# A gated mix of a state-space layer and a dense layer: a new start-up, a new order of the first stages and a split last chunk

## The chip, the cores and the metric

The kernel runs on one core of one Trainium2 chip. The metric is the device time of one execution in microseconds (us). The kernel before took 234.26 us (median of 3 runs, 233.33 to 234.62).

The core has a matrix engine (TensorE, in the profile PE, with its weight loads as PEld), VectorE (DVE), ScalarE (ACT), GpSimd (POOL) and SyncE (SP). SP, ACT and POOL issue loads; all loads run on 16 DMA engines. In what follows a "stage" is one use of TensorE on one block of 512 rows of x.

## The reference, cut to what matters

```python
g = sigmoid((x * gate_w).sum(-1, keepdims=True))             # x: 2048 x 640
# a: a diagonal complex state-space layer
Bu = einsum("bld,pd->blp", x, B_bar)                          # state projection
h[t] = Lam_bar * h[t-1] + Bu[:, t]                            # scan over 2048 steps
a = 2 * einsum("blp,dp->bld", h, C).real + x * Dskip          # output projection
# b: a dense layer
b = gelu(x @ w1 + b1) @ w2 + b2                               # 640 -> 1728 -> 640
return g * a + (1 - g) * b
```

Everything is bf16 outside and accumulates in fp32. The kernel cuts the rows into 4 blocks of 512 (`q`), 8 scan blocks of 256 (`b`) and 16 output chunks of 128 (`c`).

## The kernel before: the parts that matter here

The kernel is written as a list of operations, each with an engine, an estimated duration, the tiles that it reads and writes, and a priority. A small list scheduler, run when the kernel is built, turns this into one fixed instruction order per engine. So an engine can stand behind an operation whose data is late, even if the next one could run.

The loads, and the first block of x, which is transposed by TensorE and copied from PSUM by VectorE and ScalarE in turn:

```python
xnload(0, prio=0)                                  # x block 0, 640 KB, SyncE
W1P = [(0, 256), (256, 896), (896, F)]             # first-layer weights in three pieces, SyncE
# ... small rows of parameters on ScalarE's queue ...
load("b2",  "pool", ...)
load("dsk", "pool", "l_dsk", dsk[:, :], A_Dskip.partition_broadcast(128), ["dsk"], prio=-29, dur=1.0)
load("gwb", "pool", "l_gwb", gwb[:, :], gate_w.partition_broadcast(128), ["gwb"], prio=-28, dur=1.0)
for c in range(4):
    op(f"tp{c}", "pe", 0.5, [("xn", 0), "ident"], [("bank", bank)], f_tp, prio=-900 + c)
    op(f"tpe{c}", "dve" if c % 2 == 0 else "act", 0.6, [("bank", bank)], [("xT", 0, c)], f_tpe, prio=-900 + c)
# ... angles, sines and tables of the scan on DVE and ACT, priorities -950 to -945 ...
load_T("xT_rest", ..., prio=6)                     # 5 transposing loads, SyncE
load_T("B", ..., prio=7)                           # 10 transposing loads, SyncE
load("w2a", "sp", ..., prio=8); load("w2b", "sp", ..., prio=9)
load_T("C", ..., prio=10)                          # 10 transposing loads, SyncE
```

The stages. `m1` is the first dense layer with its gelu, `bproj` the state projection (evacuated into `U` by ScalarE), `ssm` the scan on VectorE (tiles V, W, G, result H), `gates` the dot product with the gate row, `outs` the second dense layer, the output projection and the mix:

```python
gates(0)
m1(0)
m1(1)
bproj(0)
ssm(0)
ssm(1)
xnload(1, prio=500)          # x block 1, SyncE, after all other loads
gates(1)
bproj(1)
ssm(2)
outs(0)
# ... blocks 2 and 3 ...
```

One output chunk is evacuated twice by ScalarE (E1, E2), added twice by VectorE and stored whole:

```python
t = tt(osb[c % NO][:, :], xg[c % 2][:, :], E1[c % NE][:, :], ALU.add)
E.wait("dve", t)
return tt(osb[c % NO][:, :], osb[c % NO][:, :], E2[c % NE][:, :], ALU.add)
```

## Time and profile before

| What | us | Where it is read |
|---|---|---|
| span of the profiled execution | 231.5 | head of the page |
| TensorE busy | 213.0 (92%) | part 1 |
| first matmul of the first layer | 11.24 | timeline |
| its first 7 matmuls, spacing | 0.42 to 0.43 each | stretches of one tile |
| last matmul done | 227.7 | chain |

From the page of the kernel before: the span, and the busiest engine (busy us, share, instructions).

```profile
span 231.5 us, 3235 instructions
PE 213.0 (92%) x1261; PEld 123.6 (53%) x1272; DVE 189.4 (82%) x263; ACT 102.1 (44%) x173; POOL 2.5 (1%) x11
```

A busy share of 92% says only that TensorE is the engine to watch. What TensorE needs is read from its undisturbed spacing: in the chain of waits 28 matmuls of 320 columns take 3.81 us and, elsewhere, 50 of 512 columns (49 of them recorded) take 10.8 us. Over all 768 of the one and 480 of the other that is 208 us. The rest, some 23 us, is what a change of order can win, and the waits show where it lies. The view of waits of the kernel before (who waited <- for whom: us in total, times, longest):

```profile
DVE scr L571 <- DMA xn<-in_A_x_dram: 16.8, 1, 16.8
...
ACT gth L578 <- DVE scr L571: 8.7, 3, 6.7
...
PE ps L618 <- ACT U L627: 3.9, 1, 3.9
...
PE ps L597 <- DVE xT L403: 2.7, 1, 2.7
...
PE ps L717 <- DVE H L467: 1.6, 2, 1.1
```

The first three lines are one wait seen from three engines. SyncE issued x's second block at 51.2 us, behind all transposing loads. VectorE stood 16.8 us in front of the gate product that reads it. ScalarE stood in front of the tanh of that gate. TensorE stood in front of a PSUM bank that ScalarE had yet to empty. Only the last one, 3.9 us, cost time.

The start, from the timeline of the kernel before (start, duration, engine, line, operation):

```profile
10.70 0.48 DVE L403 COPY xT<-ps 128x640 bf16<-128x640 bf16 x1
...
11.24 11.02 PE L597 MATMUL ps<-xT,W1sb 128*128 128x512 bf16 x43 [2.65 <-DVE xT L403]
```

x landed at 5.1 us, but the third of the four copies of its transpose stood behind the table work on VectorE until 10.7. And the first real matmuls are slow. From the table of stretches of the kernel before, limited to the instructions of W1's tile (stretch, its length, then busy us and count of PE and PEld, granted clock, DMA share, GB/s):

```profile
11.20:14.11 2.91, 2.87 (x7) 1.04 (x8) 1.00 1.23 282
15.20:22.00 6.80, 6.75 (x32) 3.13 (x32) 1.00 1.14 197
```

Seven matmuls in 2.87 us, later 32 in 6.75: twice the speed. The column of the granted clock reads 1.00 in both, because the first clock event in this trace is the release itself, at 14.0 us; before it the spacing is the better witness.

The end, from the chain of waits of the kernel before (start, duration, what):

```profile
224.96 2.73 PE ps L717 x20
227.69 0.02 issue
227.72 0.54 ACT E_1 L725
228.25 0.02 issue
228.28 0.50 DVE osb L467
228.78 0.02 issue
228.80 0.49 DVE osb L467
```

After the last matmul come one evacuation, two adds and a store: 3.8 us to the end of the span.

### The profile page before, as it was taken

The numbers are of one execution on the slowest core, as the hardware profiler recorded it, in microseconds if no ns is written. First come the engines' busy times: TensorE is split into PE (matmuls) and PEld (weight loads), VectorE is DVE, ScalarE is ACT, GpSimd is POOL, SyncE is SP. The second block draws the span as 40 slices with busy tenths as digits, with TensorE's granted clock in tenths as the row PEclk, the third lists the DMA queues.
The fourth block names the chain that finished last, engine by engine and source line by source line (L and its number), as shares of the span: only waits on it lengthen the run. The fifth ranks groups of instructions, "written<-read, shape, count | busy, mean of one in ns | idle before, by whom it ended". The sixth has DMA issues, their size and how long they took to land.

```text
span 231.5 us, 3235 instructions
## 1 busy us (share of the span) xinstructions
PE 213.0 (92%) x1261; PEld 123.6 (53%) x1272; DVE 189.4 (82%) x263; ACT 102.1 (44%) x173; POOL 2.5 (1%) x11
## 2 busy tenths in 40 slices
PE   1499999997599899999999999999999999999993
PEld 0344444443246676554446777644446777777772
DVE  2899997003899999999999999999996999999411
ACT  2656666551552233456553332366553332333231
POOL 4000000000000000000000000000000000000000
PEclk9999999999999999999999999999999999999999
DMA  6999599964000002200000001400000000000100
GB/s 203 325 240 184 122 115 352 169 134 120 0 0 0 3 28 57 84 31 28 0 3 0 0 31 29 142 28 0 3 0 0 3 28 28 31 0 31 57 30 28
DMA packets 29624, 15.45 MB, mean 67 GB/s; under 512 B 21802, under 2 KB 29546, under 8 KB 29610
## 3 DMA queue, kind: packets, MB, share of 16 engines
q1 hardware_dynamic: 29424, 14.91, 25.1%
q0 software_dynamic: 128, 0.33, 0.8%
q8 instruction: 10, 0.16, 0.3%
q14 instruction: 4, 0.03, 0.0%
q10 hardware_dynamic: 58, 0.01, 0.0%
HBM read 7.38 MB, written 2.62 MB: 43 GB/s over the span
## 4 chain that ended last, share of the span: by engine, by line
PE 57%; SPq 21%; DVE 16%; DMA 2%; issue 1%; ACT 1%
PE ps L693 20%; SPq L336 20%; PE ps L717 17%; PE ps L597 12%; PE ps L618 9%; DVE G L658 5%; DVE V L467 3%; DVE H L467 3%; DVE W L467 2%; DMA xn<-in_A_x_dram 2%; SPq L329 2%; DVE scr L571 1%; DVE osb L467 1%; DVE xg L733 1%; ACT U L627 0%
## 5 line engine op out<-in xcount | busy, mean ns | idle before, releaser
L597 PE MATMUL ps<-xT,W1sb 128*128 128x512 bf16 (+1 forms) x273 | 62.2, 385 | 3.0 <-DVE xT L403 2.7
L693 PE MATMUL ps<-W2sb,Gl 128*128 128x320 bf16 x448 | 63.4, 299 | 0.0
L693 PEld LDWEIGHTS ps<-W2sb,Gl 128*128 128x128 bf16 x448 | 43.8, 98 | 17.6
L604 ACT ACTIVATE Gl<-ps,b1col 128x512 bf16<-128x512 f32 (+1 forms) x56 | 38.5, 687 | 23.9 <-PE ps L597 23.9
L717 PE MATMUL ps<-CT,H 128*128 128x320 bf16 x320 | 45.9, 299 | 1.6 <-DVE H L467 1.6
L618 PE MATMUL ps<-xT,BT 128*128 128x512 bf16 x196 | 43.5, 379 | 4.2 <-ACT U L627 3.9
L597 PEld LDWEIGHTS ps<-xT,W1sb 128*128 128x128 bf16 (+1 forms) x280 | 27.4, 100 | 37.1 <-issue 3.9
L658 DVE TENSOR_TENSOR_SCAN G<-atab,V 128x1280 bf16<-128x1280 f32 x16 | 44.3, 2811 | 0.3
L717 PEld LDWEIGHTS ps<-CT,H 128*128 128x128 bf16 x320 | 31.1, 98 | 14.5 <-DVE H L467 2.4
L618 PEld LDWEIGHTS ps<-xT,BT 128*128 128x128 bf16 x200 | 19.2, 97 | 28.3 <-issue 5.6
L627 ACT ACTIVATE U<-ps 128x512 bf16<-128x512 f32 x40 | 23.3, 595 | 14.9 <-PE ps L618 14.9
L571 DVE SCALAR_TENSOR_TENSOR scr<-xn,gwb 128x640 bf16<-128x640 bf16 x16 | 13.2, 823 | 17.3 <-DMA xn<-in_A_x_dram 16.8
L701 ACT ACTIVATE E_1<-ps,g1col 128x320 bf16<-128x320 f32 x16 | 8.4, 527 | 22.0 <-PE ps L693 20.3
L701 ACT ACTIVATE E_0<-ps,g1col 128x320 bf16<-128x320 f32 x16 | 8.4, 527 | 21.8 <-PE ps L693 21.8
L725 ACT ACTIVATE E_0<-ps,gcol 128x320 bf16<-128x320 f32 x16 | 8.4, 527 | 15.1 <-PE ps L717 15.1
L467 DVE TENSOR_TENSOR V<-mr,U 128x2560 bf16<-128x2560 bf16 x8 | 11.9, 1490 | 3.1 <-ACT U L627 2.9
L733 DVE SCALAR_TENSOR_TENSOR xg<-xn,gcol,dsk 128x640 bf16<-128x640 bf16 x16 | 14.0, 883 | 0.5
L725 ACT ACTIVATE E_1<-ps,gcol 128x320 bf16<-128x320 f32 x16 | 8.4, 527 | 13.3 <-PE ps L717 13.3
L467 DVE TENSOR_TENSOR V<-V,W 128x1280 bf16<-128x1280 bf16 x16 | 12.5, 821 | 0.3
L467 DVE TENSOR_TENSOR H<-H,W 128x1280 bf16<-128x1280 bf16 x16 | 12.5, 820 | 0.3
L467 DVE TENSOR_TENSOR H<-c,G 128x2560 bf16<-128x2560 bf16 x8 | 11.9, 1487 | 0.1
L467 DVE TENSOR_TENSOR W<-s,G 128x2560 bf16<-128x2560 bf16 x8 | 11.9, 1484 | 0.0
(78 smaller groups left out, 79.9 us busy)
## 6 DMA issues: line engine op xcount, KB each, us to landing
xn<-in_A_x_dram SPq DMA_DIRECT2D x4, 640.0 KB, 4.3
out_dram<-osb SPq DMA_DIRECT2D x16, 160.0 KB, 1.8
W2sb<-in_B_w_dram SPq DMA_DIRECT2D x1, 2080.0 KB, 9.3
W1sb<-in_B_w_dram SPq DMA_DIRECT2D x1, 1040.0 KB, 10.6
W1sb<-in_B_w_dram SPq DMA_DIRECT2D x1, 800.0 KB, 8.4
W1sb<-in_B_w_dram SPq DMA_DIRECT2D x1, 320.0 KB, 4.8
dsk<-in_A_Dskip_dram POOLq DMA_DIRECT2D x1, 160.0 KB, 7.1
gwb<-in_gate_w_dram POOLq DMA_DIRECT2D x1, 160.0 KB, 7.2
```

The lines of the kernel that those rows point to most:

```text
L336: t = dma_inc("sp", nc.sync.dma_start_transpose(dst, src), sem)
L467: return inc("dve", nc.vector.tensor_tensor(out=o, in0=a, in1=b, op=o_))
L597: t = nc.tensor.matmul(PS[bank][0:n, :], W1sb[:, k, jf * 128:jf * 128 + n], xT[:, k, q * 512:(q + 1) * 512], start=(k == 0), stop=(k == KD ...
L604: return inc("act", nc.scalar.activation(Gl[q % 2][0:n, jf, :], PS[bank][0:n, :], ACT.Gelu_apprx_tanh, bias=b1col[0:n, jf:jf + 1]))
L618: t = nc.tensor.matmul(PS[bank][:, :], BT[:, kd, ci, k * 128:(k + 1) * 128], xT[:, kd, q * 512:(q + 1) * 512], start=(kd == 0), stop=(kd = ...
L627: return inc("act", nc.scalar.activation(dst, src, ACT.Copy, scale=1.0 if ci == 0 else -1.0))
L658: t = inc("dve", nc.vector.tensor_tensor_scan(out=g[:, ci, :], data0=a, data1=v[:, ci, :], initial=0.0, op0=ALU.mult, op1=ALU.add))
L693: t = nc.tensor.matmul(PS[bank][:, 0:HALF], Gl[q % 2][0:n, jf, t4 * 128:(t4 + 1) * 128], W2sb[0:n, jf, cols], start=(jf == 0), stop=(jf == ...
L701: return inc("act", nc.scalar.activation(E1[c % NE][:, cols], PS[bank][:, 0:HALF], ACT.Copy, scale=g1col[:, c:c + 1]))
L717: t = nc.tensor.matmul(PS[bank][:, 0:HALF], H[b % NHB][:, ci, k, s * 128:(s + 1) * 128], CT[:, k, ci, cols], start=(i == 0), stop=(i == 2 ...
L725: return inc("act", nc.scalar.activation(E2[c % NE][:, cols], PS[bank][:, 0:HALF], ACT.Copy, scale=gcol[:, c:c + 1]))
L733: return inc("dve", nc.vector.scalar_tensor_tensor(out=xg[c % 2][:, :], in0=xn[q % 2][:, c % 4, :], scalar=gcol[:, c:c + 1], in1=dsk[:, :] ...
```

## The change

The intent: start TensorE earlier and warm, take the late load of x's second block out of everybody's way, give the scans their input one stage sooner, and shorten the tail. The core of the diff:

```diff
-        xnload(0, prio=0)
+        for h in range(2):                                   # x block 0 in two loads
+            load(f"x0_{h}", "sp", f"l_x0{h}", xn[0][:, 2 * h:2 * h + 2, :], ...)
...
-            load(f"xn{q}", "sp", ...)                        # later blocks of x
+            load(f"xn{q}{tag}", "pool", ..., dur=1.0, lat=6.0)
...
+        def f_warm():
+            t = None
+            for _ in range(7):
+                t = nc.tensor.matmul(PS[BK_C[1]][:, :], wz[:, 0:128], wz[:, :], start=True, stop=True)
+            return inc("pe", t)
+
+        op("warm", "pe", 3.0, ["wz"], [("bank", BK_C[1])], f_warm, prio=-1000)
...
-            op(f"tpe{c}", "dve" if c % 2 == 0 else "act", 0.6, ..., prio=-900 + c)
+            op(f"tpe{c}", "dve", 0.5, [("bank", bank)], [("xT", 0, c)], f_tpe, prio=-2000 + c)
...
-        load_T("xT_rest", ..., prio=6, dur=11.7)
+        load_T("xT_rest", ..., prio=7, dur=13.0)
-        load_T("B", ..., prio=7, dur=13.1)
+        load_T("B", ..., prio=6, dur=13.1)
...
-        gates(0)
         m1(0)
-        m1(1)
         bproj(0)
         ssm(0)
+        gates(0)
+        m1(1)
         ssm(1)
-        xnload(1, prio=500)
-        gates(1)
         bproj(1)
         ssm(2)
+        xnload(1, "g")                                       # on POOL's queue, waits for nothing
+        gates(1)
         outs(0)
```

Cut here: the columns of parameters and of the bias are transposed in two operations instead of one; in blocks 2 and 3 the state projection also comes before the first layer; E1 and E2 get three buffers instead of two, G is folded into W and V; the last chunk reads its output projection straight from PSUM (`out = psum * g + E2`) and is stored in two halves; the scheduler's estimated durations are adjusted. The loads of x's blocks 2 and 3 still wait until their buffer is free.

## The prediction

> **What bounds it now.** TensorE. From 94.7 to 227.7 us the chain of waits is matmuls with nothing between them; VectorE is 98% busy there (table of stretches) but delays nothing. Undisturbed spacing, from the chain: 0.136 us per matmul of 320 columns, 0.2157 per 512. 480 x 0.2157 + 768 x 0.136 = 208 us of streaming in a 231.5 us span. The other 23 us lie in known places:
>
> - start: the first real matmul is at 11.24 us (timeline). x had landed at 5.1, but its third evacuation queued on VectorE behind table work and ended at 11.2 ("DVE xT", 2.7 us in the waits);
> - cold start: 7 matmuls take 2.9 us (0.43 apart), then 0.216: 1.4 us lost;
> - 3.9 us (56.4 to 60.3): the second state projection waits for an evacuation of U. ScalarE stood 6.7 us behind a gate's tanh, that behind the gate product on VectorE, that 16.8 us for x's second block, issued at 51.2 after all transposing loads;
> - 1.1 + 0.5 us: outputs wait for H, because that same wait held the first scan back to 60.6;
> - tail: 3.8 us after the last matmul (0.53 evacuation, two adds of 0.49, store).
>
> **What the change does.**
> 1. Transposes start on half of x; evacuations go first, all on VectorE (0.49 against 0.69 on ScalarE). First matmul at about 7.4 us: -3.8.
> 2. Seven zero matmuls, 3 us while TensorE is idle anyway. The Trainium skill ("TensorE: Matmul & The Clock Gate", Part 1) says that about 3.4 us of activity releases the clock; the trace agrees in size (2.9 us). I count -1.0, as the gap before real work may lose part.
> 3. x's later blocks go early through POOL's queue; gate work moves behind the first scans: the 3.9 us stall and the 1.6 us for H go. First scan at about 37 instead of 60.6: VectorE gets over 15 us of slack. -5.5.
> 4. The last chunk reads PSUM directly and leaves in halves: -1.0.
> 5. More E buffers, G folded into W: off the critical path.
>
> Sum -11.3. **Given back:** TensorE now runs ahead of its loads. In before the second piece of W1 landed at 10.2 us (issue plus time to landing); at a start of 7.4 it is wanted at 9.5: about +1. State projections now follow directly, so B's transposed loads are wanted at about 24 us and the rest of x at 35. In before the first of these 15 transposing loads stood 8 us at issue, the last landed about 35, the DMA being over 100% busy from 4 to 20 us. The order is swapped, not shortened, and x's second block (640 KB) joins that traffic. I expect waits of 1 to 4 us in total before the first state projection and the second first-layer stage: about +2.
>
> Net about -9: span near 222.5. **Predicted time 225 us, 80% range 221.5 to 229.5.** Faster by over 2% (under 229.6): 0.89; within 2%: 0.10; slower: 0.01.
>
> **What would show it.** First matmul with W1 at 7 to 8 us, spaced 0.216 from the start; new TensorE waits of 2 to 4 us on DMA (W1, BT, xT) before 40 us; none on ScalarE's U evacuation, none over 0.5 us on H; VectorE idle over 15 us outside its prelude; the last store under 3 us after the last matmul; matmul time unchanged.
>
> **What would make it wrong.** Transposed loads landing later than about 38 us (each us costs one; 4 us more and the gain is under 3%), or no data wait at all (222). The clock falling back in those waits (+1.4 each). Static order: a gate or an evacuation in ScalarE's or VectorE's queue ahead of its data (x's third block arriving late through POOL) brings a stall like the old one back.

## The result, and the profile after

The kernel after took 226.86 us (median of 4 runs, 225.31 to 227.38) against 234.01 us for the kernel before with the same runs. Ratios here are computed as the mean time of one kernel's fast runs over that of the other's of the same rounds, so they are not quite the ratio of the medians: 0.9684, 95% interval 0.9629 to 0.9739. One run of the kernel before in one group was slow and is left out of the ratios.

The page of the kernel after, the same lines as before:

```profile
span 225.6 us, 3268 instructions
PE 218.3 (97%) x1279; PEld 124.8 (55%) x1279; DVE 191.6 (85%) x267; ACT 101.5 (45%) x170; POOL 4.8 (2%) x14
```

TensorE is busy 5 us longer in a span that is 6 us shorter: 3.2 us of it are the zero matmuls, which do no work for the result; the rest is mostly first-layer matmuls at half speed. The chain of waits of the kernel after:

```profile
2.27 11.59 DMA W1sb<-in_B_w_dram
13.86 0.05 issue
13.91 15.23 PE ps L622 x60
29.14 10.90 PE ps L643 x50
...
220.15 2.73 PE ps L742 x20
222.88 0.03 issue
222.91 0.55 DVE osb L775
```

From 13.91 us to the end TensorE waits for nothing at all. The chain names what came before: a load of W1. The waits of TensorE in the kernel after:

```profile
PE ps L442 <- DMA W1sb<-in_B_w_dram: 1.5, 1, 1.5
PE ps L388 <- DVE wz L381: 1.2, 1, 1.2
PE ps L622 <- DVE tr L474: 1.1, 1, 1.1
PE ps L622 <- DMA W1sb<-in_B_w_dram: 0.7, 1, 0.7
```

The waits for U, for H and for the copy of x are gone. Two of these lines misname their releaser, as the inferred releasers of this view sometimes do. The first layer does not read the tile of "<- DVE tr L474". And L442 transposes the bias rows and does not read W1: the weight load just before it waited 1.7 us for b1rows. The bias rows thus came late too, at 7.5 us, but W1 came later still. When W1 came is shown by the issues of loads. From part 6 of the pages, W1's three pieces before (320, 800 and 1040 KB; the last number is us from issue to landing):

```profile
W1sb<-in_B_w_dram SPq DMA_DIRECT2D x1, 1040.0 KB, 10.6
W1sb<-in_B_w_dram SPq DMA_DIRECT2D x1, 800.0 KB, 8.4
W1sb<-in_B_w_dram SPq DMA_DIRECT2D x1, 320.0 KB, 4.8
```

and after:

```profile
W1sb<-in_B_w_dram SPq DMA_DIRECT2D x1, 1040.0 KB, 13.7
W1sb<-in_B_w_dram SPq DMA_DIRECT2D x1, 800.0 KB, 11.6
...
W1sb<-in_B_w_dram SPq DMA_DIRECT2D x1, 320.0 KB, 6.9
```

With the issue times of the timeline (1.26, 1.80, 2.36 us before; 1.76, 2.27, 2.84 after) the pieces landed at 6.1, 10.2 and 13.0 us before, and at 8.7, 13.9 and 16.5 after. The first real matmul of the kernel after starts at 8.76 us, 0.1 us after the first piece, and its third tile at 13.91, just after the second.

The granted clock and the DMA in that stretch. The table of stretches of the kernel after (stretch, length, busy us and count of PE, PEld, DVE, ACT, POOL, then granted clock, DMA share, GB/s):

```profile
5.00:6.00 1.00, 0.99 (x13) 0.68 (x13) 1.00 (x4) 0.00 (x0) 0.00 (x0) 1.00 0.86 150
6.00:7.00 1.00, 0.00 (x0) 0.00 (x0) 0.52 (x3) 0.21 (x1) 0.00 (x0) 1.00 0.73 127
7.00:8.00 1.00, 0.18 (x1) 0.09 (x1) 0.27 (x3) 0.00 (x0) 0.00 (x0) 0.87 0.99 301
...
10.00:11.00 1.00, 1.00 (x4) 0.43 (x3) 1.00 (x1) 0.00 (x0) 0.00 (x0) 0.50 1.02 389
```

Two things are to be seen. The clock falls to one half between 7 and 8 us, before the first real matmul. And from 5 to 7 us the DMA moves only 127 to 150 GB/s though its engines are 73 to 86% busy, against 389 GB/s later.

The kernel before has such a dip as well, from 6 to 8 us. Its table of stretches:

```profile
6.00:7.00 1.00, 0.38 (x7) 0.39 (x8) 0.46 (x2) 0.00 (x0) 0.00 (x0) 1.00 1.29 193
7.00:8.00 1.00, 1.00 (x12) 1.00 (x11) 0.69 (x5) 0.65 (x2) 0.00 (x0) 1.00 0.69 218
```

There it came when W1's first piece had just landed (6.1 us), and TensorE had no use for W1 before 11.2.

The clock events in the trace say the same more exactly (start, length in us, granted share; times from the span's start):

```
kernel before   14.01  218.45  1.0
kernel after     4.32    3.41  1.0
                 7.73   10.24  0.5
                17.97  208.21  1.0
```

The zero matmuls (1.20 to 4.37 us) did release the clock at 4.32 us, and it was taken back one window of 3.41 us later; TensorE had little but transposes and idle time in that window. It came back after three more windows. The Trainium skill ("TensorE: Matmul & The Clock Gate", Part 1) describes free-running windows of 3,413 ns that grant or take back the clock, and the trace agrees: 3.41 us, and 10.24 us is three times 3,413 ns. That page's Part 4 says of a transpose that "it doesn't count as PE-busy the same way". The traces agree only in part. The window from 4.3 to 7.7 us was busy for 1.8 us, nearly all of it transposes, and lost the clock, while the kernel before kept it through a window with 1.4 us of matmuls (54.97 to 58.38 us, in the wait for U). That fits the page, but the margin is small. For getting the clock back, though, transposes did count: in e8 (below) the window from 3.42 to 6.83 us held 0.95 us of zero matmuls and otherwise transposes and released the clock, while in e2 one with 2.3 us of first-layer matmuls (7.25 to 10.66 us) did not.

Where did the time go? The end of the first layer of block 0 is a good checkpoint, because both kernels do the same work up to it. The weight loads of its last tile begin at 26.72 us before and at 27.87 us after, so **in these two executions the new start-up lost 1.15 us**. All of the gain lies behind it: 3.9 us (U), 1.6 us (H) and 1.1 us (tail: 3.78 us from the last matmul to the end of the span before, 2.69 after). Less the 1.15 us, that makes 5.4 of the 5.9 us between the two spans; the rest are gaps too small to name.

The medians differ by more, 7.15 us, because the profiled execution of the kernel before was its fastest and that of the kernel after its slowest (227.38 us, granted clock 0.977; the others had 0.985 and 0.992). In e6, the same kernel traced again, the clock came back after two windows and not three, and the same point was reached at 26.11 us, 0.6 us before the kernel before. So the start-up brought between -1.15 and +0.6 us, against 3.8 us expected. Behind this point the kernel after takes 197.7 us (e6: 198.4, with one wait of 0.9) and the kernel before 204.8. The traces of e1, e2, e3, e9, e10 and e12 also take 197.7 us there, so what these runs vary is the start alone.

### The profile page after: what moved, and what is told of

It reads as the page before. It is cut to its first block, busy times and chain, and to the rows that moved or that the text cites. A ratio compares the mean times of both kernels' runs of the same rounds, so it can differ in the third digit from the quotient of the medians.

```text
span 225.6 us, 3268 instructions
## 1 busy us (share of the span) xinstructions
PE 218.3 (97%) x1279; PEld 124.8 (55%) x1279; DVE 191.6 (85%) x267; ACT 101.5 (45%) x170; POOL 4.8 (2%) x14
## 4 chain that ended last, share of the span: by engine, by line
PE 93%; DMA 5%; SPq 1%; DVE 0%; issue 0%
PE ps L718 27%; PE ps L622 27%; PE ps L742 19%; PE ps L643 19%; DMA W1sb<-in_B_w_dram 5%; SPq L328 1%; DVE osb L775 0%
## 5 line engine op out<-in xcount | busy, mean ns | idle before, releaser
L622 PE MATMUL ps<-xT,W1sb 128*128 128x512 bf16 (+1 forms) x280 | 65.8, 397 | 1.8 <-DVE tr L474 1.1
L622 PEld LDWEIGHTS ps<-xT,W1sb 128*128 128x128 bf16 (+1 forms) x280 | 28.1, 102 | 38.7 <-issue 6.6
L683 DVE TENSOR_TENSOR_SCAN W<-atab,V 128x1280 bf16<-128x1280 f32 x16 | 44.3, 2811 | 0.3
L742 PEld LDWEIGHTS ps<-CT,H 128*128 128x128 bf16 x320 | 31.3, 98 | 12.3
L652 ACT ACTIVATE U<-ps 128x512 bf16<-128x512 f32 x40 | 23.9, 597 | 19.4 <-PE ps L643 19.4
L726 ACT ACTIVATE E_0<-ps,g1col 128x320 bf16<-128x320 f32 x12 | 6.3, 527 | 16.5 <-PE ps L718 15.1
L492 DVE TENSOR_TENSOR H<-H,V 128x1280 bf16<-128x1280 bf16 x16 | 12.5, 821 | 0.3
L492 DVE TENSOR_TENSOR H<-c,W 128x2560 bf16<-128x2560 bf16 x8 | 11.9, 1489 | 0.2
L492 DVE TENSOR_TENSOR W<-mi,U 128x2560 bf16<-128x2560 bf16 x8 | 11.9, 1484 | 0.0
L492 DVE TENSOR_TENSOR V<-s,W 128x2560 bf16<-128x2560 bf16 x8 | 11.9, 1484 | 0.0
L726 ACT ACTIVATE E_1<-ps,g1col 128x320 bf16<-128x320 f32 x10 | 5.3, 528 | 13.7 <-PE ps L718 13.7
L726 ACT ACTIVATE E_2<-ps,g1col 128x320 bf16<-128x320 f32 x10 | 5.3, 527 | 13.7 <-PE ps L718 13.7
## 6 DMA issues: line engine op xcount, KB each, us to landing
W1sb<-in_B_w_dram SPq DMA_DIRECT2D x1, 1040.0 KB, 13.7
```

What stands on the lines that cost most here:

```text
L492: return inc("dve", nc.vector.tensor_tensor(out=o, in0=a, in1=b, op=o_))
L622: t = nc.tensor.matmul(PS[bank][0:n, :], W1sb[:, k, jf * 128:jf * 128 + n], xT[:, k, q * 512:(q + 1) * 512], start=(k == 0), stop=(k == KD ...
L652: return inc("act", nc.scalar.activation(dst, src, ACT.Copy, scale=1.0 if ci == 0 else -1.0))
L683: t = inc("dve", nc.vector.tensor_tensor_scan(out=g[:, ci, :], data0=a, data1=v[:, ci, :], initial=0.0, op0=ALU.mult, op1=ALU.add))
L726: return inc("act", nc.scalar.activation(E1[c % NE][:, cols], PS[bank][:, 0:HALF], ACT.Copy, scale=g1col[:, c:c + 1]))
L742: t = nc.tensor.matmul(PS[bank][:, 0:HALF], H[b % NHB][:, ci, k, s * 128:(s + 1) * 128], CT[:, k, ci, cols], start=(i == 0), stop=(i == 2 ...
```

## The experiments

The questions: what made W1 late and so ate the start-up's gain; whether the zero matmuls are worth anything; and which part of the change removed the waits for U and H. Twelve more programs ran (two of them repeats), in three groups of four; each group shares its runs of the kernel before (11 runs in each). All gave correct results.

| Run | Kernel | Median us | Ratio to before, 95% interval |
|---|---|---|---|
| | after | 226.86 | 0.9684 (0.9629 to 0.9739) |
| e1 | after, x's block 1 held back | 224.86 | 0.9608 (0.9561 to 0.9654) |
| e2 | after without zero matmuls | 226.43 | 0.9673 (0.9621 to 0.9725) |
| e3 | after with the old order | 225.37 | 0.9632 (0.9588 to 0.9675) |
| e5 | before, x's blocks through POOL | 229.32 | 0.9800 (0.9754 to 0.9846) |
| e6 | after again | 226.37 | 0.9664 (0.9628 to 0.9701) |
| e7 | after, broadcasts held back | 224.36 | 0.9577 (0.9538 to 0.9617) |
| e8 | after, both held back | 223.05 | 0.9530 (0.9495 to 0.9565) |
| e9 | e8 with the old order | 222.50 | 0.9509 (0.9474 to 0.9544) |
| e11 | e8 again | 222.66 | 0.9538 (0.9495 to 0.9580) |
| e10 | e8 without zero matmuls | 223.20 | 0.9563 (0.9515 to 0.9612) |
| e13 | e8 with the old copies of x | 223.02 | 0.9538 (0.9499 to 0.9578) |
| e12 | e9 with filler matmuls | 222.00 | 0.9490 (0.9452 to 0.9529) |

### e5: one part of the change alone, in the kernel before

```diff
-            load(f"xn{q}", "sp", f"l_xn{q}", ...)
+            load(f"xn{q}", "sp" if q == 0 else "pool", f"l_xn{q}", ...)
```

> The kernel before with one change: x's blocks 1 to 3 are loaded through POOL's queue, so block 1 at once instead of after all transposing loads. Theory: this alone takes away the 3.9 us wait for U and most of the 1.6 us for H: 4 to 5.5 us below before (about 229). W1's second piece may land at 13 to 14, which costs nothing here, as it is wanted at about 14.8. Rival (the waits come from the order of the stages): within 1 us of before.

Measured: 229.32 us, 4.9 below the 234.19 that is the median of the kernel before's fast runs in its group. By the 2% rule this is unclear (interval 0.9754 to 0.9846), but it is clear of no change. The waits of TensorE that are left in its profile:

```profile
PE ps L394 <- DMA xn<-in_A_x_dram: 5.1, 1, 5.1
PE ps L597 <- DVE xT L403: 2.7, 1, 2.7
PE ps L415 <- DMA b1rows<-in_B_b_dram: 2.0, 1, 2.0
```

All are at the start; the waits for U and for H are gone. So the earlier load of x's second block accounts for the part of the gain behind the start, but for the tail, and the order of the stages is not needed for it. (Blocks 2 and 3 moved to POOL's queue too, but in the kernel before nothing stood waiting for them: from 94.7 us on its chain is matmuls.) From the end of the first layer of block 0 this kernel takes 199.0 us, 5.7 less than the kernel before; before that point it loses 1.5 us. In this kernel the first layer starts at 12.4 us, later than in the kernel before (11.2), as the small parameter rows come later (2.0 us in the waits against 0.8 before). That fits what e1 found of the load's cost, but it is one trace each. W1's second piece landed at 12.3 us, not at 10.2, and cost nothing here, as expected.

### e3: the old order of the first stages in the kernel after

```diff
         m1(0)
+        m1(1)
         bproj(0)
         ssm(0)
         gates(0)
-        m1(1)
         ssm(1)
```

and the rest of x is again loaded ahead of B.

> The kernel after with the old order of the first stages (first layer of block 0, of block 1, then the state projection of block 0; rest of x loaded ahead of B). Theory: the earlier projection is what took away the waits for H; with the old order the first scan starts near 56 us instead of 45, TensorE waits for H again (1 to 2 us at the first output, up to 4 at the third), and the time is 2 to 5 us above after. Rival: the earlier load of x's second block alone removed those waits; then within 1 us of after.

Measured: 225.37 us. The theory fell and the rival held (0.9632 against 0.9684 and 0.9664 for the kernel after): no wait for H is in the profile, although the first scan starts at 58.4 us instead of 45.2. The first H is complete at about 69.05 us and the first output projection starts at 69.6. The fixed order had put 42 matmuls of the second layer in front of it, not 28. So the swap of the projections buys VectorE slack that is not needed here, though only 0.5 us was left without it. In this trace W1's first piece landed at 7.6 us, but the first real matmul started at 8.79: TensorE's order has the transpose of the bias rows in front, and those came late (2.4 us in the waits).

### e2: the kernel after without the zero matmuls

```diff
-        op("warm", "pe", 3.0, ["wz"], [("bank", BK_C[1])], f_warm, prio=-1000)
```

> The kernel after without the seven zero matmuls. In the profile of after the granted clock was 1.00 until 7.6 us, 0.50 from there to 18.0: the release was lost again before the first real matmul at 8.8. Theory: the zero matmuls buy nothing as long as W1 comes this late; without them the time is within 0.8 us of after. Rival (the warm-up works in most runs, the profiled one was unlucky): 1.5 to 3 us slower than after.

Measured: 226.43 us, ratio 0.9673 against 0.9684 and 0.9664 for the kernel after. As expected, they buy nothing here. In this run's profile the first ten matmuls of the first layer take 4.43 us, as in the kernel after, and end before W1's second piece lands at 14.1.

### e1: x's second block held back

```diff
-        xnload(1, "g")
+        xnload(1, "g", reads=("ptab",))     # the load waits for VectorE's tables, about 37 us
```

> The kernel after, with one change: the early 640 KB load of x's second block on POOL's queue is held back until the VectorE tables are done (about 37 us). Theory A (that load takes DMA share from W1): the second piece of W1, which landed at 13.9 us in the profile of after (10.2 in before), lands at about 11, the first piece at about 7 instead of 8.7, and the time falls by 2 to 3.5 us below after (about 224). Rival B (W1 is late because of B's transposing loads or because it is issued half a microsecond later): W1 still lands at 13 to 14 and the time is within 0.7 us of after.

Measured: 224.86 us, ratio 0.9608; against the kernel after in another group (0.9664) that is 1.3 us of 234, less than the 2 to 3.5 expected and more than the rival's 0.7. (The groups ran on different chips and the two intervals overlap; but every run of e1 is faster than every run of the kernel after.) W1's second piece landed at 11.8 us instead of 13.9. Theory A held for the second piece. It missed for the first: that piece landed at 9.9 us, later than in the kernel after, and now set the start. So x's block is not all that held W1 up: in the kernel before the two pieces landed at 6.1 and 10.2 us.

The packet records of the trace, which tell of each transfer its queue, size, start and duration, showed a candidate. POOL's queue carries, in this order, the broadcasts of the skip row and of the gate row (each one row of 1.25 KB written to 128 partitions, 160 KB) and x's second block. Both appear as packets of 5,120 bytes:

```
kernel after, packets of 5,120 bytes on POOL's queue
broadcasts:        64 packets,  4.64 to  9.10 us, mean 431 ns, longest 1,156 ns
x's second block: 128 packets,  8.89 to 12.83 us, mean 203 ns, longest   371 ns
```

A packet of a broadcast took twice as long, on average, as a packet of the same size of x. Between 4 and 7 us, while they ran, the core moved 127 to 206 GB/s. That the first 64 packets are the broadcasts is inferred from their order and number (320 KB over 5,120 bytes). The place in time does not explain the difference: in e7 (below), where the two changed places, x's packets took 214 ns on average from 5.6 us on and the broadcasts' 382 ns from 38.7 us on.

One thing the packet records also show: the broadcasts are not new. The kernel before issues them at the same time, and its 64 packets run from 5.90 to 9.43 us, 460 ns on average. New is that they now start before W1's first piece has landed: the two kernels with the old start-up have the piece at 6.1 us (e5: 6.0) and the first broadcast packet at 5.9 (5.7), while in the kernel after and e1 to e3 the packets start at 4.6 to 5.1 and the piece lands at 7.6 to 9.9. What moved them forward (x in two loads, W1 issued half a microsecond later, the other order of the transposing loads) was not varied by a run of its own.

### e6, e7, e8: the broadcasts held back, alone and with x's block

e6 is the kernel after, unchanged.

> The kernel after itself, unchanged, as the reference of this group on this chip: about 226.8 us, ratio to before near 0.968; W1's second piece lands between 13 and 14 us in its profile, and the clock record shows a release after the zero matmuls that is lost before the first real matmul.

Measured: 226.37 us, ratio 0.9664. W1's second piece landed at 13.7 us, and the clock was released at 4.33 us, lost at 7.75 and back at 14.57.

e7 moves the two broadcast loads behind the tables; x's block stays early:

```diff
-        load("dsk", "pool", "l_dsk", ..., prio=-29, dur=1.0)
-        load("gwb", "pool", "l_gwb", ..., prio=-28, dur=1.0)
+        load("dsk", "pool", "l_dsk", ..., prio=-29, dur=1.0, lat=7.0, reads=("ptab",))
+        load("gwb", "pool", "l_gwb", ..., prio=-28, dur=1.0, lat=7.0, reads=("ptab",))
```

> The kernel after, with the two broadcast loads (the skip row and the gate row, each 1.25 KB spread over 128 partitions) held back until VectorE's tables are done; x's second block stays early. The packet records of after show 64 packets of 5,120 bytes on POOL's queue between 4 and 8 us that take 0.2 to 0.95 us each, 0.2 us being what the same size costs for x's block later; while they run the core moves 130 to 200 GB/s instead of 390. Theory C (the broadcasts hold W1 up): the dip from 5 to 8 us goes, W1's first piece lands near 6.5 to 7 us and the second near 11 to 12, TensorE's first real matmul starts near 7 to 7.5, and the time is 1.5 to 3.5 us under after. Rival (the dip has another cause, such as the 512-byte rows of W1's first piece): first matmul still after 8.3, time within 0.8 us of after.

Measured: 224.36 us, 2.0 us below e6. The second piece landed at 10.9 us. The first landed at 8.2 us and the first real matmul was at 8.25, so this part of the expectation missed: x's block, now alone on POOL's queue, had moved up to where the broadcasts had been (its packets run from 5.6 us on). And a new wait appeared, the one that the prediction had looked for, 1.6 us for B:

```profile
PE ps L643 <- DMA BT<-in_A_B_im_dram: 1.6, 1, 1.6
```

e8 holds back both.

> The kernel after with both the broadcasts and x's second block held back until the tables are done. Theory: W1's pieces land near 6.5, 9 and 11.5 us, so the first layer of block 0 runs without a stop from about 7 us; then the next limit shows, B's transposed loads, which by the SyncE issue times land near 24 to 25, a wait of 1 to 3 us before the first state projection; net 3 to 5.5 us under after (about 222). Rival (start-up is bounded by something else, such as the cold clock or the bias column): within 1.5 us of the run that holds back only x's block.

Measured: 223.05 us, 3.3 us below e6 (ratios 0.9530 and 0.9664). The three pieces landed at 7.1, 9.2 and 11.8 us and the first layer starts at 7.37. The same rows of the table of stretches as above, for e8:

```profile
5.00:6.00 1.00, 1.00 (x13) 0.80 (x10) 0.92 (x2) 0.00 (x0) 0.00 (x0) 1.00 0.97 177
6.00:7.00 1.00, 0.90 (x9) 0.59 (x8) 0.75 (x3) 0.21 (x1) 0.00 (x0) 1.00 0.95 330
7.00:8.00 1.00, 0.63 (x3) 0.31 (x4) 0.93 (x6) 0.41 (x2) 0.00 (x0) 1.00 1.06 382
```

From 6 us on the core moves 330 GB/s and more until 11 us. The first clock event of this trace is the release, at 6.83 us (the 1.00 in the rows before it is a default), and it is not lost again. So what POOL had issued, the broadcasts and x's second block together, is what kept W1 late in the kernel after: without it the second piece lands even earlier than in the kernel before (10.2 us). Of the two only x's block was added by the change. The kernel before would perhaps gain from later broadcasts too; no run tested that. The low rate from 5 to 6 us stays also without them, so it has another cause; W1's first piece, whose rows are only 512 bytes long, is moving then, but no run tested that.

The expected wait for B was 1 to 3 us. In e8's list of TensorE's waits it does not stand; 0.4 us of it is in that of e11, the same kernel. Two waits put down to ScalarE, 0.9 and 0.7 us, are what is left of the start. Before the first one ScalarE loads its function tables. The second is right in front of the state projection, and B is only just hidden behind it: B's last load landed at 24.25 us, the gelu of the first layer's last tile ended at 24.51.

### e9: both held back, with the old order

> The same as the run before it, with the old order of the first stages (first layer of block 1 before the first state projection, rest of x loaded ahead of B). Theory: loads land in time in this order (rest of x by about 20 us, wanted at 22), so the wait for B goes; but VectorE gets its first work some 15 us later, and waits for H of 0 to 3 us can come back. Between 1.5 us faster and 2 us slower than the run before it.

Measured: 222.50 us, within the noise of e8 (the intervals of 0.9509 and 0.9530 overlap). No wait for H came back, and no wait for a load is left after the start. In the profiled run the clock was released at 4.31 us, lost at 7.72 and back at 11.13; eight or nine real matmuls ran at half speed in between.

### e10, e11, e13: what the zero matmuls and the copies are worth once W1 is on time

e11 is e8 unchanged.

> The kernel that holds back the broadcasts and x's second block, unchanged, as the reference of this group: ratio to before near 0.953, granted clock 1.00 throughout after the zero matmuls.

Measured: 222.66 us, ratio 0.9538. In one of its six runs the granted clock averaged 0.992, so the release can still be lost.

e10 takes the zero matmuls away from it.

> The same without the seven zero matmuls. In the unchanged after they bought nothing, since W1 came too late for the released clock. Theory: with W1 on time they do pay: without them the first 7 or more matmuls with W1 run 0.43 us apart and the time is 1 to 2 us above the reference of this group. Rival (they are worthless anyway, transposes or the first real work release the clock as early): within 0.5 us.

Measured: 223.20 us, ratio 0.9563 against 0.9538: 0.6 us, inside the noise. The theory of 1 to 2 us is not borne out. Its trace shows where the gain ends. Without the zero matmuls the clock came at 10.31 us instead of 5.15, and the first layer lost time. Yet the first state projection starts at 24.34 us in e10 and at 24.39 in e11. From the waits of TensorE in e11:

```profile
PE ps L622 <- ACT Gl L629: 1.0, 1, 1.0
...
PE ps L643 <- DMA BT<-in_A_B_im_dram: 0.4, 1, 0.4
```

With a warm start TensorE just runs into ScalarE and into B's loads sooner.

e13 gives e8 the old copies of x (VectorE and ScalarE in turn, at the old priority).

> The reference of this group with the old evacuation of x (halves shared by VectorE and ScalarE, behind the table work in VectorE's order; x still loaded in two parts). Theory: now that W1 is on time, the evacuation is what the first real matmul waits for: it moves from 7.4 to 9 to 11 us and the time rises by 1.5 to 3.5 us, part of it lost again to the cold clock, part hidden where B's loads are the limit. Rival (W1 still sets the start): within 0.7 us.

Measured: 223.02 us, ratio 0.9538, the same as e11. The expectation missed, and the reason is in the timeline: in this program the fixed order put all four copies ahead of the angle work anyway (the last one ends at 7.39 us, first real matmul at 7.49), probably because the parameters are now transposed after most of x and not before it. So e13 did not bring back the late copy of the kernel before. That the copies cost the kernel before 2.7 us is read from its waits; it was not tested by a run.

### e12: a filler, and the fastest version

Filler on top of e9, between the last transpose of x and the bias column (the expectation's clock times for e9 are 0.3 us later than those above, which count from the span's start):

```diff
+        def f_fill():
+            t = None
+            for _ in range(6):
+                t = nc.tensor.matmul(PS[BK_C[1]][:, :], wz[:, 0:128], wz[:, :], start=True, stop=True)
+            return inc("pe", t)
+
+        op("fill", "pe", 2.0, ["wz"], [("bank", BK_C[1])], f_fill, prio=-896.5)
```

> The run with both loads held back and the old order, plus six more zero matmuls between the last transpose of x and the bias column, to keep TensorE busy until W1 lands. In that run's profile the clock release of 4.6 us was lost at 8.0 and came back at 11.4, so that ten or more real matmuls ran at half speed. Theory: the filler keeps the release, 1 us under the run without it (ratio about 0.947), clock record 1.00 in nearly all runs. Rival: no change, or up to 0.5 us slower as the filler delays real work.

Measured: 222.00 us (220.97 to 222.28), ratio 0.9490. The whole list of TensorE's waits in its profile:

```profile
PE ps L388 <- DVE wz L381: 1.2, 1, 1.2
```

That is the wait of the very first zero matmul; after it TensorE has work to the end. The granted clock was 0.999 or 1.00 in all six runs, while e9 had two runs of six at 0.992. Against e9 the gain (0.9490 and 0.9509, in different groups) is inside the noise. Against both kernels of this study it is not: the interval ends at 0.9529, and those of the kernel after begin at 0.9628. It is the fastest version that ran. The tail was not varied by a run of its own; its 1.1 us is read from the traces: e5, which has the old one, ends 3.81 us after its last matmul, the kernels with the new one 2.70 or 2.71 us.

## Why the prediction was right or wrong

The predicted time was 225.0 us, the measured one 226.86, inside the range of 221.5 to 229.5; the direction was right and the predicted gain of some 9 us was 7.15. (The written terms add up to -8.3, not to the -9 given there.) Point by point:

- **What bounds the kernel (right).** TensorE, and the 208 us of streaming. After 13.9 us the chain of the kernel after is nothing but matmuls.
- **Step 3, the waits for U and H, -5.5 us (right in size; the credit was shared wrongly).** Both are gone. The prediction credited the early load together with the later gate work and the earlier first scan. e5 shows that the early load alone gives 4.9 us of total time, and e3 that the earlier scan is not needed. VectorE's first scan work was put at 37 us instead of 60.6; it came at 40.7 (at 35.9 in e8, whose start is early).
- **Step 4, the tail, -1.0 us (right).** 3.78 to 2.69 us.
- **Step 1, the first matmul at 7.4 us, -3.8 us (wrong).** It started at 8.76, when W1's first piece landed (6.1 in the kernel before). The prediction counted x's copies only and did not ask when this piece would come.
- **Step 2, the clock, -1.0 us (wrong).** The release came and was lost again; some 20 real matmuls ran at half speed in the profiled execution instead of 7. About half of them were hidden behind the wait for W1's second piece. The prediction had named this as a risk, for another wait.
- **Given back: W1, +1 us (the term that was mis-sized).** The second piece was put at 10.2 us, as in the kernel before. It landed at 13.9. The prediction had named x's 640 KB as new traffic, but only charged it to the transposing loads. e1 shows that x's block alone put this piece back by 2.1 us (13.9 to 11.8). For the rest the broadcasts are the witness, which now run into W1's first piece, though what moved them there was not varied: with both held back the piece lands at 9.2, and the time is 3.3 us lower (e8 against e6).
- **Given back: B and the rest of x, +2 us (wrong in the profiled execution of the kernel after, zero there).** TensorE arrived so late that these loads were on time. (In e6, which was faster to that point, TensorE stood 0.9 us in front of the first state projection. The view puts this down to ScalarE, and for the weight load to B, which landed at 28.0 us.) The wait does exist: as soon as the broadcasts were held back it showed, 1.6 us in e7.
- **VectorE idle over 15 us (right).** From its first scan work to the last matmul VectorE is idle for 23.9 us in the kernel after, against 9.9 in the kernel before.

So the start-up was expected to give 3.8 us at the checkpoint (steps 1 and 2, less the wait for W1), and it cost 1.15 us there in the profiled execution (it gave 0.6 us in e6). The 2 us charged to B and x made up for part of that error, and the other steps came in as predicted. So that the total came out 1.9 us from the prediction is in part luck: two errors with opposite signs.

## What to carry to other kernels

When a change lets an engine start earlier, list every load in flight at that time, on all queues, and ask which of them is needed first: here a load that was merely early on another queue put the one that was needed back by 2.1 us, and a small load took twice the time per packet that its bytes suggested. The clock that the warm-up had won here was lost in the gap before the first real work (after, e6, e9), and a filler kept it (e12): if that work is late, fill the gap too. Before you name a loss of 1 us from one trace, see where that execution stands among the others and trace it again. And after removing a wait look for the next one behind it, since a gain at the start may end in a later load and not in the total.

## What the Trainium skill lacked or had wrong

- "DMA: Bandwidth & Descriptors", section "Issuing engines are not separate DMA queues", says that issuing from several engines saves only the sequencer's time. It says that they interleave, but not what that can cost a load that is needed first, here 2.1 us (e1). The same page's section "Queues, rings and completion order" says that each DMA engine goes round-robin between queues by packets, which fits what was seen: between 9 and 10 us in the kernel after POOL's queue moved 261 KB and SyncE's 139 KB, and holding POOL's loads back brought W1's second piece forward from 13.7 to 9.2 us (e6 and e8).
- No page was found that gives the cost of loading one row into 128 partitions. Here a packet of 5,120 bytes of such a load took 431 ns on average and up to 1,156 ns, against 203 ns for the same size of an ordinary load (kernel after), and late in e7 382 ns. Why is open.
- "TensorE: Matmul & The Clock Gate", Part 1, agrees with the clock events here (windows of 3.41 us). The page's closing table advises a warm-up before benchmarking; what it lacks for kernels is that a warm-up of 3.2 us was granted 3.41 us of full clock and then cost nothing and gave nothing (e2: 0.9673 against 0.9664), and that six more zero matmuls across the gap kept it (e12: 0.999 or 1.00 in six of six runs).
- The same page does not say how busy a window must be. In the 14 traces here (windows counted in steps of 3,413 ns from the clock events) every window at half clock in which TensorE was busy, transposes included, for 2.77 us or more of its 3.41 released the clock, and none did with 2.69 us or less.
- The same page's Part 4, on transposes, holds here only in part: they counted towards the release (e8, window from 3.42 to 6.83 us, 0.95 us of zero matmuls and otherwise transposes).
- No page was found on how long a transposing load can occupy its issuing engine: the first one stood 8.0 us on SyncE behind W1 in the kernel before, 7.6 us in the kernel after and 3.3 us in e8.
